# Two head groups' last query-weight rows in one block, no idle products between stages, and thirty small transfers in the queue

## The chip, the core and the metric

One core of a Trainium2 chip runs the whole kernel as one program. The metric is the device time of one execution in microseconds (us), the median of several runs; lower is better. The core has five engines that matter here: PE (TensorE, matrix products; PEld is its weight load), DVE (VectorE), ACT (ScalarE), POOL (GpSimd) and SP (SyncE), which in this kernel does nothing but issue transfers. The transfers themselves run on the core's 16 DMA engines.

## The reference

A decoder step of four tokens (B = 4) of width D = 448: pre-normalised attention against a cache, then a pre-normalised MLP.

```python
x = A_x                                             # (4, 1, 448)
h = x + attention(layernorm(x), k_cache, v_cache, wq, wo)
h2 = h + mlp(layernorm(h), w1, b1, w2, b2)          # returned

# attention: 16 query heads, 8 key/value heads, head size 256,
# only the last W = 1024 of 4096 cache positions are read
q = (x @ wq).reshape(4, 1, 16, 256)                 # wq is (448, 4096)
p = softmax(q . k / 16); o = p . v
return o.reshape(4, 1, 4096) @ wo                   # wo is (4096, 448)

# mlp: layernorm once more, gelu(y @ w1 + b1) @ w2 + b2, with 1792 hidden units
```

With four tokens there is little arithmetic. What is large is the data: every byte of the read cache positions and of the weights (all in float32) is used once, 88.23 MB read by the profile's count.

## The kernel before

The work is cut by the 8 key/value heads, called groups here. Each group needs its keys, its values, 512 columns of `wq` and 512 rows of `wo`. The host packs them into arrays, all but one with 128 rows (one for each partition of the on-chip memory), so that one transfer brings a block of long rows. There are three slots of on-chip memory (`ring`, line 213), used in turn: `t0`, `l1`, `l2`, `l3` and so on. Groups are treated in pairs ("stages" n = 0 to 3): `both_queries` projects the queries of both groups of a pair into one accumulator, `scores` multiplies them with the keys, `softmax` follows on DVE and ACT, `transpose_p` turns the probabilities, `values` multiplies them with the values, and `outputs` adds the product with `wo` to `acc`. Stage boundaries follow the transfers: after each load `l1` to `l8` the program computes what that load made possible. The last pair and the MLP (arrays `k7`, `vo`, `v7`, `wo`, `w1`, `w2`) form a tail with finer transfers: `w1` in two pieces, `w2` in four pieces of falling size.

Order and waits. The kernel is recorded by a small layer (`Machine`, line 78): each engine gets its instructions in the order in which the code is written, and each instruction waits for the semaphores of those it depends on. All transfers are issued by SP, in the order of the code, into one hardware queue. A transfer into a slot first waits until PE has read the slot's old contents. In the profile nearly every instruction has line 74, the layer's recording line, so one goes by names: `slot<-l` is a load of `l1` to `l8`; `b_s` are the scores, `b_o` the values' products (late in the program also the fill and the last products), `b_m` projections and transposes, `b_acc` the output products, `b_t` transposed probabilities and idle products.

The last 64 rows of `wq`. 448 is 3 times 128 plus 64. For one group, `packed` (line 740) puts the first 384 rows into three blocks of 512 columns, and the last 64 rows into a fourth block of 256 columns, its left half on partitions 0 to 63 and its right half on 64 to 127. So `wq_parts` (line 239) makes five products for a group: three of 512 columns, and two of 256 columns, for which the normalised input `yT` has an extra fifth chunk. Group 1 is different: its three full blocks come with `k0`, and its last 64 rows come by two transfers of their own, `wq1` into `wq1_last` (lines 457 to 460), 64 KB each, read from a source with 8 rows of 4 times 512 numbers each.

Idle products. `keep_warm_between` (line 444) runs six products of a zeroed bfloat16 tile into an unused accumulator. It stands behind seven of the stages (after `l1` to `l7`). Other idle and fill products (`keep_warm`, `fill`) stand in the tail.

Of the kernel before, what the change touches and what calls it, by code (L numbers as in the profile page):

```python
# [5 lines left out]
F32 = mybir.dt.float32  # L6
# [5 lines left out]
B, D = 4, 448  # L12
HQ, HKV, SK, DH = 16, 8, 4096, 256
# [3 lines left out]
P = 128  # L17
H = P // 2
ND = 4
# [3 lines left out]
Q = 32  # L23
CACHE = NKC * B * DH
HALF = CACHE // 2
WEIGHTS = 4 * D
SLOT = CACHE + 2 * WEIGHTS + HALF
COLUMNS = ND * B + 4 + 4 * 4
# [3 lines left out]
GRANULE = 4  # L32


class Memory:
# [9 lines left out]
    def part(self, ap):  # L45
        if self.psum:
            return slice(0, 1), np.zeros(1, int)
        pairs = list(ap.ap)
        first, at = divmod(ap.offset, self.row)
        rows = slice(first // GRANULE, -(-(first + pairs[0][1]) // GRANULE))  # L50
# [148 lines left out]

def block_kernel(nc, wq0, k0, wq1, l1, l2, l3, l4, l5, l6, l7, l8, k7, vo, v7, wo, w1, w2, out):  # L200
    real, nc = nc, Machine(nc)
# [53 lines left out]
    def output_weights(t):  # L255
# [6 lines left out]
        out=ident, in_=ident, compare_op=ALU.not_equal, fill=1.0, base=0, pattern=[[-1, P]], channel_multiplier=1  # L262
# [11 lines left out]

    yz = const.tile([P, ND + 1, B + Q], F32, name="yT")
    nc.vector.memset(yz, 0.0)
    yT = [yz[:, :, B:], yz[:, :, :Q]]
    wq1_last = const.tile([H, 512], F32, name="wq1_last")
    zT = const.tile([P, ND, Q], F32, name="zT")
# [42 lines left out]

    def project(pq, parts, start):
        for j, y, cols, w in parts:
            nc.tensor.matmul(
                pq[j * Q : (j + 1) * Q, cols], y, w,
                start=start and cols.start == 0, stop=not start and cols.stop == 512,
            )

# [123 lines left out]
    wqt, xT, b2T, b1T = cut(load(t, 0, wq0), (WEIGHTS, ND * B, 4, 4 * 4))  # L453
    wqt = wq_parts(yT[0], wqt)
    xT = xT.rearrange("p (a b) -> p a b", a=ND)
    ka, kb, wqt1 = cut(load(t, WEIGHTS + COLUMNS, k0), (HALF, HALF, 3 * 512))
    for i in range(2):
        nc.sync.dma_start(
            wq1_last[i * Q : (i + 1) * Q, :], wq1[i].rearrange("e (p c) -> e p c", c=512)[:, :4, :]
        )  # L460
    d = work.tile([P, ND, B], F32, tag="d", name="d_x")
# [7 lines left out]
    nc.vector.tensor_mul(yT[0][H:, 4, :B], d[H:, 3, :], rx[H:, :])  # L469
    pq = pq_tile(0)  # L470
    project(pq, wqt, True)

# [13 lines left out]

    project(pq, wq_parts(yT[1], wqt1, wq1_last), False)
    queries(0, pq)
# [22 lines left out]
    keep_warm_between()  # L511

# [3 lines left out]
    outputs(0, po, rec, (wo_a, wo_b))  # L516
    keep_warm_between()

    wq_a, wq_b, ka, kb, k2 = cut(load(slot("l3"), 0, l3), (WEIGHTS, WEIGHTS, HALF, HALF, HALF))
    both_queries(1, (wq_a, wq_b))  # L520
# [4 lines left out]
    keep_warm_between()  # L525

    k2, v, wq_a, wq_b = cut(load(slot("l4"), 0, l4), (HALF, CACHE, WEIGHTS, WEIGHTS))
    scores(s, 1, 1, keys(k2))
    p, sums = softmax(1, s)
    both_queries(2, (wq_a, wq_b))  # L530
    rec = transpose_p(1, p, sums)
    po = po_tile(1)
    values(0, chunks(v), po)
    keep_warm_between()

# [4 lines left out]
    outputs(1, po, rec, (wo_a, wo_b))  # L540
    keep_warm_between()

# [5 lines left out]
    rec = transpose_p(2, p, sums)  # L548
    keep_warm_between()

    v, va, wq_a, wq_b = cut(load(slot("l7"), 0, l7), (CACHE, HALF, WEIGHTS, WEIGHTS))
    po = po_tile(2)
    values(0, chunks(v), po)
    values(1, chunks(va), po, range(0, 2))
    both_queries(3, (wq_a, wq_b))
    keep_warm_between()

# [238 lines left out]
```

## Time and profile before

| what | value |
|---|---|
| time before, median of 3 runs | 211.98 us (211.97 to 212.29) |
| the profiled execution's own time | 212.03 us |
| its span, first to last instruction | 210.7 us |
| PE busy | 138.5 us (66%) |
| DVE busy, ACT busy | 28.8 us, 14.4 us |
| share of the time of 16 DMA engines taken by the main queue | 97.5% |
| bytes moved, mean rate over the span | 88.42 MB, 420 GB/s |
| mean granted TensorE clock | 0.862 |

The page lists, for each engine, how long it was busy, and for the DMA queue how long its packets took as a share of what 16 engines could have spent. The chain of waits goes back from the last instruction: at each step to what released it. A view by stretches of time ("windows") gives the same busy times and the DMA share for any part of the span. Issue rows (SPq) give when SP issued a transfer, and how long the issue took; landing times run from the issue to the last part on chip.

### The profile page before, as it was taken

Reading aid. Unit: us, or ns where it says so; the run is one execution under the profiler, and the core shown is the slowest. Engines: PE = TensorE matmul, PEld = TensorE weight load, DVE = VectorE, ACT = ScalarE, POOL = GpSimd, SP = SyncE. Lnnn points to the kernel's source line nnn. Section 1 sums busy time; section 2 is a strip of 40 time slices with the busy share of each in tenths; the row PEclk is TensorE's granted clock in tenths of the full one; section 3 lists DMA queues with packets and bytes.
Section 4 is the critical chain, followed back from the end, with each engine's and each line's share of the span. In section 5 each row is a group of like instructions: output and inputs, shape, how many; then the busy total and the mean of one; then the engine's idle time right before and its main releaser. Section 6 shows DMA issues by size and latency. Waiting matters only on the chain.

```text
span 210.7 us, 2189 instructions
## 1 busy us (share of the span) xinstructions
PE 138.5 (66%) x976; PEld 47.2 (22%) x976; DVE 28.8 (14%) x135; ACT 14.4 (7%) x34; POOL 5.0 (2%) x17
## 2 busy tenths in 40 slices
PE   0557869621971676098459577619806999888996
PEld 0420212200220221023112111202301223224332
DVE  7210101300020011013002003200100213012320
ACT  2010000200000010011000000200100002010311
POOL 5100000000000000000000000000000000000100
PEclk9999996985697599769969958757975899999999
DMA  7999999899999999999999999999999999999993
GB/s 296 428 399 473 448 491 389 386 411 530 398 398 410 530 389 410 410 518 398 413 411 448 481 398 437 398 494 398 446 392 448 416 428 429 437 398 452 412 410 131
DMA packets 3256, 88.42 MB, mean 420 GB/s; under 512 B 368, under 2 KB 624, under 8 KB 1200
## 3 DMA queue, kind: packets, MB, share of 16 engines
q1 hardware_dynamic: 3248, 88.30, 97.5%
q8 instruction: 7, 0.11, 0.2%
q14 instruction: 1, 0.01, 0.0%
HBM read 88.23 MB, written 0.07 MB: 419 GB/s over the span
## 4 chain that ended last, share of the span: by engine, by line
DMA 78%; PE 17%; SPq 2%; DVE 1%; issue 1%; ACT 0%
DMA slot<-l 64%; DMA slot<-w 14%; PE b_o L74 9%; PE b_s L74 4%; PE b_acc L74 3%; SPq L74 2%; PE b_m L74 1%; DVE oT L74 1%; DVE w_o L74 0%; PE b_t L74 0%; DVE o_u L74 0%; ACT o_u L74 0%; DVE o_res L74 0%
## 5 line engine op out<-in xcount | busy, mean ns | idle before, releaser
L74 PE MATMUL b_o<-slot,pT 128*32 128x512 f32 x224 | 32.3, 729 | 26.3 <-DMA slot<-l 25.6
L74 PE MATMUL b_s<-slot,qT 128*32 128x512 f32 x256 | 38.7, 760 | 14.3 <-DMA slot<-l 12.9
L74 PE MATMUL b_m<-slot,yT 128*32 128x512 f32 (+1 forms) x76 | 11.4, 705 | 11.4 <-DMA slot<-l 6.2
L74 PEld LDWEIGHTS b_s<-slot,qT 128*32 128x32 f32 x256 | 9.4, 136 | 40.8 <-issue 23.9
L74 PEld LDWEIGHTS b_o<-slot,pT 128*32 128x32 f32 x224 | 7.7, 130 | 47.5 <-DMA slot<-l 28.0
L74 PE MATMUL b_t<-idle 128*32 128x512 bf16 x64 | 17.7, 397 | 0.5 <-DVE pT L74 0.5
L74 DVE TENSOR_REDUCE w_mx<-b_s 128x1 f32<-128x512 f32 x8 | 5.5, 691 | 49.5 <-PE b_s L74 49.5
L74 ACT ACTIVATE o_p<-b_s,w_nm 128x512 f32<-128x512 f32 x8 | 5.4, 682 | 96.4 <-DVE w_nm L74 96.4
L74 DVE TENSOR_SCALAR w_o<-b_o,w_rec 128x512 f32<-128x512 f32 x4 | 3.0, 751 | 50.2 <-PE b_o L74 50.2
L74 PEld LDWEIGHTS b_m<-slot,yT 128*32 128x32 f32 x76 | 4.2, 140 | 17.8 <-DMA slot<-l 6.7
L74 PEld LDWEIGHTS b_t<-idle 128*32 128x32 bf16 x64 | 5.9, 99 | 9.9 <-issue 5.2
L74 PE MATMUL b_t<-ident,o_p 128*128 128x128 f32 x32 | 5.0, 283 | 4.0 <-ACT o_p L74 3.9
L74 PE MATMUL b_acc<-slot,oT 128*32 128x448 f32 x52 | 6.1, 546 | 1.9 <-DVE oT L74 1.9
L74 DVE TENSOR_REDUCE w_sm<-b_m 128x32 f32<-128x128 f32 x4 | 1.2, 291 | 44.8 <-PE b_m L74 44.8
L74 ACT COPY w_qs<-b_m 128x512 f32<-128x512 f32 x4 | 2.3, 584 | 58.0 <-PE b_m L74 58.0
L74 POOL TENSOR_TENSOR o_r<-w_ve,mhalf 128x1 f32<-128x1 f32 x2 | 1.1, 542 | 189.3 <-DVE w_ve L74 189.3
L74 PEld LDWEIGHTS b_t<-ident,o_p 128*128 128x128 f32 x32 | 3.4, 141 | 7.4 <-ACT o_p L74 7.4
L74 PE MATMUL b_m<-ident,w_qs 128*128 128x128 f32 x16 | 3.1, 324 | 3.0 <-ACT w_qs L74 3.0
L74 PE MATMUL b_m<-slot,mean 128*128 128x12 f32 (+1 forms) x4 | 1.1, 371 | 5.4 <-DMA slot<-wq 5.4
L74 PE MATMUL b_o<-slot,yT 128*32 128x512 f32 x10 | 4.6, 595 | 0.0
L74 PE MATMUL b_m<-ident,w_o 128*128 128x128 f32 x20 | 3.3, 287 | 1.8 <-DVE w_o L74 1.8
L74 DVE COPY pT<-b_t 128x16 f32<-128x16 f32 x32 | 3.3, 167 | 5.9 <-PE b_t L74 5.9
(94 smaller groups left out, 66.3 us busy)
## 6 DMA issues: line engine op xcount, KB each, us to landing
slot<-l SPq DMA_DIRECT2D x6, 7936.0 KB, 43.7
slot<-l SPq DMA_DIRECT2D x2, 6144.0 KB, 35.3
slot<-k SPq DMA_DIRECT2D x1, 4864.0 KB, 15.7
slot<-vo SPq DMA_DIRECT2D x1, 4544.0 KB, 32.9
slot<-k SPq DMA_DIRECT2D x1, 4096.0 KB, 40.9
slot<-v SPq DMA_DIRECT2D x1, 3072.0 KB, 18.8
slot<-w SPq DMA_DIRECT2D x1, 2240.0 KB, 28.4
slot<-w SPq DMA_DIRECT2D x1, 1792.0 KB, 33.8
```

The source lines that it names most:

```text
L74: self.machine.add(Op(self.name, lambda: getattr(issuer, what)(*args, **kwargs), outs, ins, what))
```

## The change

Three things are changed.

- **Query weights.** The last 64 rows of both groups of a pair are now stacked into one block of 128 rows and 512 columns (`last`). `yT` loses its fifth chunk; its fourth chunk now holds the last 64 inputs on partitions 0 to 63 in the columns of the first group and on partitions 64 to 127 in those of the second, so one product (`wq_last`) serves both groups. A pair takes 7 products instead of 10. For pair 0 the block comes with `wq0`, which grows from 1828 to 2084 columns. `wq1`, `wq1_last` and their two transfers are gone. The number of bytes of the weights is the same.
- **Idle products.** `keep_warm_between` and its seven calls are gone, 42 products.
- **Small transfers.** `spread` issues 15 transfers: of 15 rows with 19 numbers, 14 rows with 18, and so on to 1 row with 5, from `l1` into an otherwise unused tile `aside`. It is called after the load of `k0`, and again after the two pieces of `w1` and before those of `w2`. POOL clears `aside` near the end, which makes it wait for the second fifteen; what POOL had to do before that is done by then in program order, and no other instruction waits for this clearing.

A fourth edit makes the recording layer's bookkeeping of partitions use the step of an access as well as its count.

```diff
-    def wq_parts(y, t, last=None):
-        parts = [(a, y[:, a, :], slice(0, 512), t[:, a * 512 : (a + 1) * 512]) for a in range(3)]
-        if last is not None:
-            return parts + [(3, y[:H, 3, :], slice(0, 512), last)]
-        for i in range(2):
-            parts.append((3, y[:, 3 + i, :], slice(i * 2 * P, (i + 1) * 2 * P), t[:, 3 * 512 :]))
-        return parts
+    def wq_parts(y, t):
+        return [(a, y[:, a, :], t[:, a * 512 : (a + 1) * 512]) for a in range(3)]
+
+    def wq_last(t):
+        return [(3, yT[0][:, 3, :], t)]
...
-    def keep_warm_between():
-        warm = ps_t.tile([P, 512], F32, tag="t", name="between")
-        keep_warm(6, warm)
...
+    aside = const.tile([16, 180], F32, name="aside")
+
+    def spread():
+        at = 0
+        for n in range(15, 0, -1):
+            nc.sync.dma_start(aside[:n, at : at + 4 + n], l1[:n, : 4 + n])
+            at += 4 + n
...
-    ka, kb, wqt1 = cut(load(t, WEIGHTS + COLUMNS, k0), (HALF, HALF, 3 * 512))
-    for i in range(2):
-        nc.sync.dma_start(
-            wq1_last[i * Q : (i + 1) * Q, :], wq1[i].rearrange("e (p c) -> e p c", c=512)[:, :4, :]
-        )
+    ka, kb, wqt1 = cut(load(t, QUERY + 512 + COLUMNS, k0), (HALF, HALF, QUERY))
+    spread()
...
         for g in range(2):
-            project(pq, wq_parts(yT[g], wqs[g]), g == 0)
+            project(pq, wq_parts(yT[g], wqs[g]), g == 0, g == 1)
+        project(pq, wq_last(wqs[2]), True, True)
         queries(n, pq)
...
     w1t = cut(load(e[0], CACHE, w1, (2 * F + F // 2, F)), (F, F, F // 2, F))
+    spread()
     w2t = cut(load(e[2], CACHE, w2, (8 * D, 3 * D, 2 * D, D)), NFC * (D,))
...
+    nc.gpsimd.memset(aside, 0.0)
```

On SP at the start of the program, where `wq`, `k` and `l` are the loads of `wq0`, `k0` and of `l1`, `l2`, there stood before:

```order
L74 DMA slot<-wq 128x1828 [waits barrier_Pool_Activation_PE_DVE_SP_release]
L74 DMA slot<-k 128x9728
L74 DMA wq_last<-wq 32x1x512 x2
L74 DMA slot<-l 128x12288
L74 DMA slot<-l 128x15872
```

With the change the start of SP's order is:

```order
L76 DMA slot<-wq 128x2084 [waits barrier_Pool_Activation_PE_DVE_SP_release]
L76 DMA slot<-k 128x9728
L76 DMA aside<-l 15x19
L76 DMA aside<-l 14x18
L76 DMA aside<-l 13x17
...
L76 DMA aside<-l 2x6
L76 DMA aside<-l 1x5
L76 DMA slot<-l 128x12288
L76 DMA slot<-l 128x15872
```

Fifteen issues, none of which waits, stand ahead of `l1` where two stood before.

On SP in the tail, where the two pieces of `w1` are followed by the first of `w2` (3584 columns), stands with the change:

```order
L76 DMA slot<-w 128x1792
L76 DMA aside<-l 15x19 [waits landed_28]
L76 DMA aside<-l 14x18 [waits landed_29]
...
L76 DMA aside<-l 2x6 [waits landed_41]
L76 DMA aside<-l 1x5 [waits landed_42]
L76 DMA slot<-w 128x3584
L76 DMA slot<-w 128x1344 [waits done_PE]
```

Each of the fifteen waits for its namesake of the first call, since it writes the same place; before, the row of 3584 columns followed the one of 1792 directly.

On PE after the outputs of pair 0 (`b_acc`), where the load of `l3` is waited for, there stood before:

```order
L74 MATMUL b_acc<-slot,oT 32x448 x3
L74 MATMUL b_t<-idle 32x512 x6
L74 MATMUL b_m<-slot,yT 32x512 [waits landed_191]
L74 MATMUL b_m<-slot,yT 32x512 x2
L74 MATMUL b_m<-slot,yT 32x256 x2
L74 MATMUL b_m<-slot,yT 32x512 x3
L74 MATMUL b_m<-slot,yT 32x256 x2
```

and with the change:

```order
L76 MATMUL b_acc<-slot,oT 32x448 x3
L76 MATMUL b_m<-slot,yT 32x512 [waits landed_190]
L76 MATMUL b_m<-slot,yT 32x512 x6
L76 MATMUL b_m<-ident,w_qs 128x128 [waits done_ACT]
```

The six idle products ahead of the wait are gone, and the ten projections behind it are seven.

More of the change, by code (lines that the diff above doesn't have):

```diff
@@ L26 @@
 WEIGHTS = 4 * D
+QUERY = 3 * 512
 SLOT = CACHE + 2 * WEIGHTS + HALF
@@ L49, in part @@
         first, at = divmod(ap.offset, self.row)
-        rows = slice(first // GRANULE, -(-(first + pairs[0][1]) // GRANULE))
+        end = first + pairs[0][0] // self.row * (pairs[0][1] - 1) + 1
+        rows = slice(first // GRANULE, -(-end // GRANULE))
         cols = np.zeros(1, int)
@@ L197, in tile, with block_kernel @@
         return flat.rearrange(f"p ({names}) -> p {names}", **{f"a{i}": n for i, n in enumerate(shape[1:])})
-def block_kernel(nc, wq0, k0, wq1, l1, l2, l3, l4, l5, l6, l7, l8, k7, vo, v7, wo, w1, w2, out):
+def block_kernel(nc, wq0, k0, l1, l2, l3, l4, l5, l6, l7, l8, k7, vo, v7, wo, w1, w2, out):
     real, nc = nc, Machine(nc)
@@ L320, in rsqrt, with project @@
         nc.gpsimd.tensor_tensor(dst, ve, mhalf[: dst.shape[0], : dst.shape[1]], op=ALU.pow)
[L323 to L327, printed above, removed]
-            )
+    def project(pq, parts, start, stop):
+        for j, y, w in parts:
+            nc.tensor.matmul(pq[j * Q : (j + 1) * Q], y, w, start=start, stop=stop)
     def pq_tile(n):
@@ L442, in keep_warm @@
             nc.tensor.matmul(warm[:Q], idle[:, :Q], idle, start=True, stop=True)
[L444 to L446 removed]
     def po_tile(g, pool=ps_o, tag="o"):
         return pool.tile([P, 2, DH], F32, tag=tag, name=f"po{g}")
+    aside = const.tile([16, 180], F32, name="aside")
[4 more added lines that the diff above has]
+            at += 4 + n
     t = slot("t0")
[L453 to L454 removed]
+    wqt, wq_both, xT, b2T, b1T = cut(load(t, 0, wq0), (QUERY, 512, ND * B, 4, 4 * 4))
     xT = xT.rearrange("p (a b) -> p a b", a=ND)
[L456 to L460 removed]
+    ka, kb, wqt1 = cut(load(t, QUERY + 512 + COLUMNS, k0), (HALF, HALF, QUERY))
+    spread()
     d = work.tile([P, ND, B], F32, tag="d", name="d_x")
@@ L468, in block_kernel @@
     nc.vector.tensor_mul(yT[0][:H, 3, :B], d[:H, 3, :], rx[:H, :])
-    nc.vector.tensor_mul(yT[0][H:, 4, :B], d[H:, 3, :], rx[H:, :])
+    nc.vector.tensor_mul(yT[0][H:, 3, B : 2 * B], d[H:, 3, :], rx[H:, :])
     pq = pq_tile(0)
-    project(pq, wqt, True)
+    project(pq, wq_parts(yT[0], wqt), True, False)
+    project(pq, wq_last(wq_both), True, True)
     wide = t[:, SLOT - 6 * P :].rearrange("p (n j q) -> p n j q", n=6, j=4)
@@ L516, in block_kernel @@
     outputs(0, po, rec, (wo_a, wo_b))
-    keep_warm_between()
-    wq_a, wq_b, ka, kb, k2 = cut(load(slot("l3"), 0, l3), (WEIGHTS, WEIGHTS, HALF, HALF, HALF))
-    both_queries(1, (wq_a, wq_b))
+    wq_a, wq_b, wq_c, ka, kb, k2 = cut(load(slot("l3"), 0, l3), (QUERY, QUERY, 512, HALF, HALF, HALF))
+    both_queries(1, (wq_a, wq_b, wq_c))
     s = score_tiles(1)
@@ L524, in block_kernel @@
     scores(s, 1, 0, keys(k2))
-    keep_warm_between()
-    k2, v, wq_a, wq_b = cut(load(slot("l4"), 0, l4), (HALF, CACHE, WEIGHTS, WEIGHTS))
+    k2, v, wq_a, wq_b, wq_c = cut(load(slot("l4"), 0, l4), (HALF, CACHE, QUERY, QUERY, 512))
     scores(s, 1, 1, keys(k2))
     p, sums = softmax(1, s)
-    both_queries(2, (wq_a, wq_b))
+    both_queries(2, (wq_a, wq_b, wq_c))
     rec = transpose_p(1, p, sums)
@@ L540, in block_kernel @@
     outputs(1, po, rec, (wo_a, wo_b))
-    keep_warm_between()
     kb, ka, k2 = cut(load(slot("l6"), 0, l6), (HALF, HALF, HALF))
@@ L548, in block_kernel @@
     rec = transpose_p(2, p, sums)
-    keep_warm_between()
-    v, va, wq_a, wq_b = cut(load(slot("l7"), 0, l7), (CACHE, HALF, WEIGHTS, WEIGHTS))
+    v, va, wq_a, wq_b, wq_c = cut(load(slot("l7"), 0, l7), (CACHE, HALF, QUERY, QUERY, 512))
     po = po_tile(2)
@@ L745, in packed @@
         return np.concatenate([full, last], axis=-1)
-    wq = packed(np.asarray(A_wq).reshape(D, HKV, 512).transpose(1, 0, 2))
+    wq = np.asarray(A_wq).reshape(D, HKV // 2, 2, 512)
+    whole = wq[: 3 * P].reshape(3, P, HKV // 2, 2, 512).transpose(2, 3, 1, 0, 4).reshape(HKV, P, QUERY)
+    last = wq[3 * P :].transpose(1, 2, 0, 3).reshape(HKV // 2, P, 512)
+    wq = [np.concatenate([whole[2 * n], whole[2 * n + 1], last[n]], axis=1) for n in range(HKV // 2)]
     wo = np.asarray(A_wo).reshape(HKV, 4, P, D).transpose(0, 2, 1, 3).reshape(HKV, P, 4 * D)
@@ L761 @@
     loads = {f"l{i + 1}": np.concatenate(parts, axis=1) for i, parts in enumerate(loads)}
-    k0 = np.concatenate([k[0], wq[1][:, : 3 * 512]], axis=1)
-    wq1 = np.asarray(A_wq).reshape(D, HKV, 512)[3 * P :, 1].reshape(2, 8, 4 * 512)
-    wq1 = np.concatenate([wq1, np.zeros((2, 8, 512), np.float32)], axis=2)
+    k0 = np.concatenate([k[0], whole[1]], axis=1)
     vo = np.concatenate([v[6], wo[6, :, : 2 * D]], axis=1)
@@ L782 @@
     arrays = {
-        "wq0": np.concatenate([wq[0], xT, b2, b1], axis=1), "k0": k0, "wq1": wq1, **loads, "k7": k[7], "vo": vo, "v7": v[7], "wo": wo_end, "w1": w1, "w2": w2,
+        "wq0": np.concatenate([whole[0], last[0], xT, b2, b1], axis=1), "k0": k0, **loads, "k7": k[7], "vo": vo, "v7": v[7], "wo": wo_end, "w1": w1, "w2": w2,
     }
```

16 lines of the change are left out of this document (6 added, 10 removed).

## The prediction

> **What bounds the kernel now.** First the page, for which resource is full.
>
> ```profile
> span 210.7 us, 2189 instructions
> PE 138.5 (66%) x976; PEld 47.2 (22%) x976; DVE 28.8 (14%) x135; ACT 14.4 (7%) x34; POOL 5.0 (2%) x17
> q1 hardware_dynamic: 3248, 88.30, 97.5%
> q8 instruction: 7, 0.11, 0.2%
> DMA 78%; PE 17%; SPq 2%; DVE 1%; issue 1%; ACT 0%
> ```
>
> The main queue takes 97.5% of what 16 DMA engines have, 205.4 us of 210.7; no compute engine comes near. So I read the DMA share by stretches of time (columns: stretch, length, PE, PEld, DVE, ACT and POOL busy, TensorE clock, DMA share, GB/s).
>
> ```profile
> 0.00:1.70 1.70, 0.00 (x0) 0.00 (x0) 0.55 (x4) 0.97 (x1) 1.10 (x8) 1.00 0.00 0
> 17.00:100.00 83.00, 52.35 (x330) 16.34 (x334) 8.66 (x46) 4.54 (x11) 0.00 (x0) 0.84 1.00 432
> 100.00:200.00 100.00, 71.99 (x520) 23.68 (x513) 12.83 (x57) 6.09 (x15) 0.83 (x2) 0.85 0.99 428
> 206.00:206.50 0.50, 0.50 (x12) 0.10 (x4) 0.00 (x0) 0.00 (x0) 0.00 (x0) 1.00 0.89 351
> 206.50:207.00 0.50, 0.50 (x20) 0.27 (x16) 0.00 (x0) 0.02 (x1) 0.00 (x0) 1.00 0.49 197
> 207.00:207.50 0.50, 0.50 (x24) 0.29 (x12) 0.00 (x0) 0.50 (x1) 0.00 (x0) 1.00 0.47 183
> 207.50:208.00 0.50, 0.50 (x21) 0.36 (x21) 0.00 (x0) 0.01 (x1) 0.00 (x0) 1.00 0.26 97
> 208.00:209.00 1.00, 0.73 (x24) 0.24 (x15) 0.19 (x1) 0.00 (x0) 0.00 (x0) 1.00 0.00 0
> ```
>
> Nothing moves for the first 1.7 us; then the engines run without a gap at 432 GB/s, 27.0 GB/s each. At the end the share falls in two steps: half of the engines stop near 206.5, the other half go on until about 207.9. The late half sets the end, since a transfer has landed when its last engine is done:
>
> ```profile
> 207.94 0.79 PE L74 MATMUL b_o<-slot,gT_last 128*4 128x64 f32 x16
> 208.34 0.11 PEld L74 LDWEIGHTS b_o<-slot,gT_last 128*4 128x4 f32 x8 [0.21 <-DMA slot<-w]
> 208.81 0.29 DVE L74 TENSOR_TENSOR o_res<-b_o,o_hb 128x128 f32<-128x128 f32 x1 [4.40 <-PE b_o L74]
> 209.13 0.35 SPq L74 DMA_DIRECT2D out<-o_res  x1
> ```
>
> The last products wait for the last piece of `w2`; half a microsecond later the sum and the output transfer follow. So the time is the finish of the latest engine plus a tail of about 2.8 us. Anything else counts only if it leaves the queue empty.
>
> **The change, part by part.**
>
> *Idle products and fewer projections.* The queue runs far ahead of PE. From the chain of waits (start, us, what), and two issue rows:
>
> ```profile
> 62.94 44.94 DMA slot<-l
> 117.41 42.44 DMA slot<-l
> 168.93 0.80 SPq L74 DMA_DIRECT2D slot<-v  x2
> slot<-v SPq DMA_DIRECT2D x1, 3072.0 KB, 18.8
> ```
>
> A load issued at 62.94 lands 44.9 us later, but its 7,936 KB (8.13 MB) need only 18.8 us at 432 GB/s; so it stood 26 us in the queue, and PE may free a slot that much later. At 117.41 it is 23.6 us. The tightest is `v7`: 18.8 us for 3.15 MB that need 7.3, so 11.5 us. Against that:
>
> ```profile
> 151.32 1.47 PE L74 MATMUL b_t<-idle 128*32 128x512 bf16 x6
> 159.89 3.64 PE L74 MATMUL b_o<-slot,pT 128*32 128x512 f32 x16 [7.10 <-DMA slot<-l]
> 180.50 3.64 PE L74 MATMUL b_o<-slot,pT 128*32 128x512 f32 x32 [0.54 <-DMA slot<-vo]
> ```
>
> After six idle products PE waits 7.10 us, and its next 16 products take 228 ns each where, after a wait of 0.54 us, 32 take 114 ns each. The clock is lost in the wait with the idle products as it will be without them. If one more stage went cold, 16 products would cost 1.8 us, inside 11.5. I cost both edits at 0; the cover is that slack.
>
> The Trainium skill's "TensorE: Matmul & The Clock Gate", Part 1, says that the clock halves after an idle window of about 3.4 us, which speaks against taking idle products out; the trace agrees on the halving, 228 against 114 ns, and by the rule the 7.10 us wait is cold either way.
>
> *Query weights on the engines.* The two removed transfers are 64 KB each, 131 KB together; the bytes now ride with `wq0`, which has 128 rows. At 27.0 GB/s that is 0.30 us on each of 16 engines. Read from 8 source rows, they lay either on 8 engines, 0.61 us on each of those, or on 16. So a late engine gets +0.30 (it had none), -0.30 (it had them), or 0. Which engines are late is the question. One cause is seen around 36 us:
>
> ```profile
> q8 instruction: 1, 0.02, 4.2%
> ```
>
> In the 1.4 us from 35.5 to 36.9 one instruction fetch takes 4.2% of 16 engines' time: 0.94 us of one engine. There are seven of these and one more on another queue, about as many as there are late engines. No row says which engines fetch. With fetches on engines that also carried the small parts I would expect a third step of 0.61 us in the fall of the share; I see two. So I take the side of the cost, at half its size: +0.15.
>
> The skill's "DMA: Bandwidth & Descriptors", section on why a DMA increments its semaphore by 16, says that a transfer runs on the largest number up to 16 that divides both sides' outer sizes, on the lowest-numbered engines: 8 for the removed pair, n for a small transfer of n rows. No row here shows the numbers of engines.
>
> *Small transfers on the engines.* The nearest row is the output, 128 packets of 512 B and 16 semaphore writes in 0.5 us:
>
> ```profile
> DMA packets 144, 0.07 MB, mean 131 GB/s; under 512 B 16, under 2 KB 144, under 8 KB 144
> q1 hardware_dynamic: 144, 0.07, 46.8%
> ```
>
> 46.8% of 16 times 0.5 us is 3.74 us, 26 ns a packet; 19 of them are 512 B at 27.0 GB/s, 7 ns are fixed. A row of 20 to 76 B is then 10 ns, with its semaphore write 17. An engine that has a row of all thirty gets 0.51 us, one with none 0; if each packet cost the full 26 ns, 1.56. On average an engine has 240 / 16 = 15 rows, 0.26 us. I take 0.20 for the late ones.
>
> *SP's time.* Issues (start, us they took), their durations (min/median/max ns), and landings after the issue:
>
> ```profile
> 0.74 0.39 SPq L74 DMA_DIRECT2D slot<-wq  x1
> 1.18 0.41 SPq L74 DMA_DIRECT2D slot<-k  x1
> 1.64 1.55 SPq L74 DMA_DIRECT2D wq_last<-wq  x2
> 170.25 0.96 SPq L74 DMA_DIRECT2D slot<-w  x2
> L74 SPq DMA_DIRECT2D wq_last<-wq x2: 682/750/819, 1.6 to 2.5; - x2
> L74 SPq DMA_DIRECT2D slot<-l x8: 327/328/499, 3.2 to 117.4; - x8
> slot<-k SPq DMA_DIRECT2D x1, 4864.0 KB, 15.7
> slot<-w SPq DMA_DIRECT2D x1, 896.0 KB, 30.1
> ```
>
> Fifteen issues at 0.33 to 0.82 us are 4.9 to 12.3 us, so `l1` is issued between 6.5 and 13.9 instead of 1.64 + 1.55 = 3.2. `k0` occupies the queue until 1.2 + 15.7 = 16.9, and first bytes came 1.0 us after the first issue (0.74 to 1.7): hidden by at least 2 us. In the tail, where the two pieces of `w1` are issued from 170.25 to 171.2, the fifteen end by 171.2 + 12.3 = 183.5 while the second piece lands at about 170.7 + 30.1 = 200.8: hidden. Both at 0.
>
> *Fewer instructions.* 42 idle products and 22 others of PE go, each with a weight load: 128 of 1952 instructions. Seven fetches for 1952 make one per 260 to 280, so at most one fetch fewer; the end is set by the latest of eight engines, and seven remain. 0, at best -0.94.
>
> **The sum**, against the profiled execution: 212.03 + 0.15 + 0.20 = 212.4. The median lies 0.05 under the profiled time, so **212.3 us**. This case alone spans 211.7 (-0.30, no cost of small rows) to 213.2.
>
> **Rivals.**
>
> *A. The queue takes a limited number of transfers (slower).* The last piece of `w2` took 7.34 us to issue:
>
> ```profile
> 172.73 7.34 SPq L74 DMA_DIRECT2D slot<-w  x1
> slot<-k SPq DMA_DIRECT2D x1, 4096.0 KB, 40.9
> slot<-vo SPq DMA_DIRECT2D x1, 4544.0 KB, 32.9
> ```
>
> `k7`, issued at 128.7, had landed by then (169.6). Nine others were outstanding (`vo`, two of `v7`, `wo`, two of `w1`, three of `w2`), and it was let in at 180.07, when `vo`, issued at 147.50, was ending. If nine is the limit whatever their size, the fifteen fill the queue behind `k0`: when it ends the last six and `l1` are still to be issued, 7 times 0.4 to 0.75 us plus 1.0 for first bytes, 3.8 to 6.3 us of empty engines, and the same again before `w2`. That is +7.6 to +12.6, about 221 us. Against it: `vo` landed at 147.50 + 32.9 = 180.4, after the issue had ended, so the limit is not on transfers that have not landed; a limit on queued rows fits too (eight whole transfers of 8 rows per engine, 64), and 30 small rows beside two or six large transfers pass it without a gap. It decides if fewer than 16 transfers may wait behind `k0`.
>
> *B. The issue is dearer than any row shows (slower).* From 1.64 to 16.2 there are 14.6 us for fifteen: it decides from 0.97 us each. At 1.2, `l1`'s first bytes come at 20.6 instead of 17.2: +3.4, 215.4. The dearest row is 0.82.
>
> *C. The late half moves up (faster).* If the late engines are those that carried the small parts (-0.30), the last fetch falls behind the last load, and small rows lie on the engines that have time, the second step shrinks from 1.4 us towards the mean, 0.7: 211.3. For it: the share shows that half the engines idle 1.4 us at the end. Against it: no part of the change takes a fetch off a late engine before the last.
>
> *D. The clock counts after all.* If `l8`'s stage went so cold that `v7` came 11.5 us later, +1.8 for the next cold 16 products: 214. Only the 7.10 us wait speaks on it, and against it.
>
> **How the numbers follow.** A measurement here tells 0.2%, 0.42 us, from no change. The forecast's case has 0.60: of it 0.40 within 0.42 us, 0.18 slower, 0.02 faster. C has 0.22, 0.19 of it faster. A 0.10, B 0.06 and D 0.02 are slower. Together: faster 0.21, same 0.43, slower 0.36. The range 211.2 to 213.8 leaves out A, nearly all of B, and the far end of C, 0.18.
>
> **What would show it.** Right: the DMA share stays 1.00 from 5 to 200 us; `l1` is issued before 14 us; the share still falls in two steps, ending near 208.3; PE's waits before loads grow by about 1.5 us and nothing else moves. Wrong: a share under 0.9 around 17 us or 200 us (A or B, told apart by whether the small issues take long from the first or only from the eighth); a single step at the end (C); a `v7` issued after 180 us (D).

## The result, and the profile after

The changed kernel takes 215.82 us (median of 4 runs, 215.18 to 216.56) against 212.09 us before (211.97 to 212.29). The ratio is 1.0178, 95% interval 1.016 to 1.0197: slower by 3.7 us, and outside the predicted range of 211.2 to 213.8. The profiled execution is the fastest of the four, 215.18 us, with a span of 213.9 us.

The page after (engines, queues, and the chain by engine):

```profile
span 213.9 us, 2100 instructions
PE 130.2 (61%) x912; PEld 41.8 (20%) x912; DVE 28.8 (13%) x135; ACT 14.4 (7%) x34; POOL 5.2 (2%) x18
q1 hardware_dynamic: 3648, 88.31, 97.0%
q8 instruction: 7, 0.11, 0.2%
DMA 73%; PE 15%; SPq 9%; issue 1%; DVE 1%
```

PE has 8.3 us less to do and the bytes are the same, yet the span is 3.2 us longer. The DMA engines are still the bound. The end of the kernel after, first by stretches (columns as in the prediction, DMA share and GB/s last), then its last waits and products:

```profile
208.00:208.50 0.50, 0.21 (x4) 0.19 (x8) 0.00 (x0) 0.00 (x0) 0.00 (x0) 1.00 0.88 348
208.50:209.00 0.50, 0.50 (x8) 0.13 (x4) 0.00 (x0) 0.00 (x0) 0.00 (x0) 1.00 0.51 204
209.50:210.00 0.50, 0.50 (x16) 0.17 (x12) 0.00 (x0) 0.00 (x0) 0.00 (x0) 1.00 0.28 111
210.00:210.50 0.50, 0.50 (x24) 0.40 (x16) 0.00 (x0) 0.45 (x1) 0.00 (x0) 1.00 0.18 68
210.50:211.00 0.50, 0.50 (x18) 0.20 (x16) 0.00 (x0) 0.09 (x1) 0.00 (x0) 1.00 0.09 32
211.00:211.50 0.50, 0.50 (x21) 0.29 (x19) 0.00 (x0) 0.00 (x0) 0.00 (x0) 1.00 0.00 0
```

```profile
208.29 1.71 PE L76 MATMUL b_acc<-slot,gT 128*32 128x448 f32 x16 [1.96 <-DMA slot<-w]
211.09 0.80 PE L76 MATMUL b_o<-slot,gT_last 128*4 128x64 f32 x16
212.28 0.35 SPq L76 DMA_DIRECT2D out<-o_res  x1
```

Before, the share fell in two steps and was gone by 208.0. After, half of the engines stop at about 208.5, and from there it runs down a staircase: 0.51, 0.28, 0.18, 0.09. That is eight late engines, then about four, three, one or two. The last of them finishes near 211. PE waits 1.96 us for the first piece of `w2`, a wait that was too short to be listed before. The last products start at 211.09 instead of 207.94, 3.15 us later, and the tail behind them is 2.8 us as it was. So the loss lies in when the data arrive.

Where did it arise? The share of busy time doesn't tell, but the bytes do. Two stretches that hold the two sets of small transfers, before and then after:

```profile
15.00:22.00 7.00, 4.36 (x11) 0.97 (x12) 0.00 (x0) 0.58 (x1) 0.00 (x0) 1.00 1.00 431
198.00:206.00 8.00, 7.52 (x63) 2.89 (x65) 1.76 (x7) 1.75 (x5) 1.08 (x2) 1.00 1.00 421
```

```profile
15.00:22.00 7.00, 3.24 (x14) 1.10 (x18) 0.70 (x5) 0.59 (x1) 0.00 (x0) 1.00 1.06 407
198.00:206.00 8.00, 7.54 (x58) 3.01 (x56) 2.21 (x10) 2.69 (x7) 1.33 (x3) 1.00 1.00 373
```

All four have a share of 1.00 or above. But the second stretch moved 373 GB/s instead of 421: 48 times 8 us is 0.38 MB less, 0.9 us of all engines at 432 GB/s. So the time that was lost counts as busy. (The view puts a packet with all its bytes and all its time where the packet starts, and a packet of a large load takes up to 2.3 us, so such a stretch can be some per cent off and a share can pass 1.00. Where it matters below, a figure from the trace's packet records is given, in which each packet is spread over its own duration.)

What SP did in the kernel after (issue rows: start, us; then durations of the thirty, min/median/max ns; then KB and us from issue to landing), and PE's waits for loads:

```profile
1.62 5.60 SPq L76 DMA_DIRECT2D aside<-l  x15
7.26 0.83 SPq L76 DMA_DIRECT2D slot<-l  x2
172.05 11.60 SPq L76 DMA_DIRECT2D aside<-l  x15
183.70 9.75 SPq L76 DMA_DIRECT2D slot<-w  x4
L76 SPq DMA_DIRECT2D aside<-l x30: 253/341/2688, 1.6 to 182.8; - x30
slot<-l SPq DMA_DIRECT2D x1, 6144.0 KB, 26.4
slot<-w SPq DMA_DIRECT2D x1, 1792.0 KB, 24.5
161.08 3.64 PE L76 MATMUL b_o<-slot,pT 128*32 128x512 f32 x16 [8.89 <-DMA slot<-l]
```

`l1` is issued at 7.26 and lands at 7.26 + 26.4 = 33.7; before it was 3.23 + 28.5 = 31.7. So it comes 1.9 us later though it was issued long before its turn. `l8` ended PE's wait at 161.08 instead of 159.89, 1.2 us later: of the first delay 0.7 us is made up again on the way. The first piece of `w2` lands at 183.70 + 24.5 = 208.2.

### The profile page after: what moved, and what is told of

Its sections match the earlier page's. It is cut to its first block, busy times and chain, and to the rows that moved or that the text cites. A ratio compares the mean times of both kernels' runs of the same rounds, so it can differ in the third digit from the quotient of the medians.

```text
span 213.9 us, 2100 instructions
## 1 busy us (share of the span) xinstructions
PE 130.2 (61%) x912; PEld 41.8 (20%) x912; DVE 28.8 (13%) x135; ACT 14.4 (7%) x34; POOL 5.2 (2%) x18
## 4 chain that ended last, share of the span: by engine, by line
DMA 73%; PE 15%; SPq 9%; issue 1%; DVE 1%
DMA slot<-l 61%; DMA slot<-w 11%; SPq L76 9%; PE b_o L76 9%; PE b_acc L76 3%; PE b_s L76 2%; PE b_m L76 1%; DVE oT L76 1%; DVE w_o L76 0%; DVE o_res L76 0%
## 5 line engine op out<-in xcount | busy, mean ns | idle before, releaser
L76 PE MATMUL b_o<-slot,pT 128*32 128x512 f32 x224 | 34.3, 768 | 31.1 <-DMA slot<-l 30.2
L76 PE MATMUL b_s<-slot,qT 128*32 128x512 f32 x256 | 39.1, 766 | 17.4 <-DMA slot<-l 16.0
L76 PE MATMUL b_m<-slot,yT 128*32 128x512 f32 x56 | 11.7, 839 | 12.8 <-DMA slot<-l 7.8
L76 PE MATMUL b_t<-idle 128*32 128x512 bf16 x22 | 6.6, 382 | 0.0
L76 PEld LDWEIGHTS b_m<-slot,yT 128*32 128x32 f32 x56 | 2.3, 137 | 18.7 <-DMA slot<-l 8.6
L76 PEld LDWEIGHTS b_m<-ident,w_qs 128*128 128x128 f32 x16 | 2.3, 179 | 8.6 <-ACT w_qs L76 8.6
## 6 DMA issues: line engine op xcount, KB each, us to landing
slot<-w SPq DMA_DIRECT2D x1, 1792.0 KB, 24.5
```

The source lines that it names most:

```text
L76: self.machine.add(Op(self.name, lambda: getattr(issuer, what)(*args, **kwargs), outs, ins, what))
```

## The experiments

The theory formed on the trace of after: each small transfer holds every engine that it uses for a fixed time of about 0.2 us, whatever its rows (their landings step by about that much). What was still to be told apart was which part of the change costs what, whether it goes by transfers, by rows or by the length of a row, and what the query block and the idle products do by themselves. Each time stands beside runs of the kernel before on the same chip (212.00 to 212.12).

### Without the small transfers, and with one set of them

The changed kernel without both calls:

```diff
-    spread()
...
-    spread()
...
-    nc.gpsimd.memset(aside, 0.0)
```

> The changed kernel without its thirty small transfers: the query block and the missing idle products alone. Theory S (the small transfers are the whole loss, each holding an engine for about 0.19 us, as their landings 17.41, 17.59, 17.79 ... 19.98 us step): 211.7 to 212.4 us, like before. Rival Q (the bytes moved to all engines and the colder PE are part of the loss, the 1.15 us by which every load between l2 and w1 lands later): 213.1 to 213.6 us.

Measured: 212.71 us (7 runs), ratio 1.0029 [1.0017, 1.004]. The small transfers cost 215.82 - 212.71 = 3.1 us of the 3.7; the rest of the change costs 0.6, more than was expected. The wait for the first piece of `w2` is nearly gone:

```profile
206.36 1.71 PE L76 MATMUL b_acc<-slot,gT 128*32 128x448 f32 x16 [0.19 <-DMA slot<-w]
```

With the second call alone:

```diff
     ka, kb, wqt1 = cut(load(t, QUERY + 512 + COLUMNS, k0), (HALF, HALF, QUERY))
-    spread()
```

> The changed kernel with the fifteen small transfers before w2 alone. Theory S: the loads up to w1 land as before, the four pieces of w2 2 us later: 213.9 to 214.4 us. Rival Q: loads up to w1 already 1.15 us late, 215.0 to 215.6 us.

With the first call alone:

```diff
     w1t = cut(load(e[0], CACHE, w1, (2 * F + F // 2, F)), (F, F, F // 2, F))
-    spread()
...
-    nc.gpsimd.memset(aside, 0.0)
```

> The changed kernel with the fifteen small transfers behind k0 alone. Theory S: l1 lands 2 us late, l2 and all later loads 1.1 to 1.2 us late, because some of the instruction fetches then fall on engines that are ahead: 213.0 to 213.5 us. Rival Q: the same time, but for another reason, which the run without any small transfers tells apart. Rival D (delays add in full, nothing is absorbed): 214.0 to 215.0 us.

Measured: 213.8 us (ratio 1.0089 [1.0056, 1.0122]) and 213.71 us (1.0074 [1.0059, 1.0089]). Each call alone costs 1.0 to 1.1 us, both together 3.1; both times lie just outside what theory S had said (213.9 to 214.4 and 213.0 to 213.5). The five runs of the second call alone spread from 213.21 to 215.35, so its price is known to about half a microsecond at best. The stretches show the same loss of bytes, and it stands where the call is. Without small transfers, with the first call alone (15 to 22), with the second alone (198 to 206):

```profile
15.00:22.00 7.00, 2.91 (x10) 0.87 (x10) 0.55 (x5) 0.71 (x2) 0.00 (x0) 0.71 1.05 456
198.00:206.00 8.00, 7.54 (x57) 3.00 (x56) 2.14 (x9) 2.69 (x7) 1.09 (x2) 1.00 0.99 412
```

```profile
15.00:22.00 7.00, 3.04 (x10) 0.91 (x10) 0.56 (x5) 0.59 (x1) 0.00 (x0) 0.65 1.02 399
```

```profile
198.00:206.00 8.00, 7.07 (x54) 2.60 (x52) 1.98 (x9) 2.08 (x5) 1.33 (x3) 1.00 0.99 368
```

456 - 399 over 7 us is 0.40 MB, 0.92 us of all engines; 412 - 368 over 8 us is 0.35 MB, 0.81 us. With the packets spread over their durations it is 434 against 382 and 421 against 380 GB/s, 0.84 and 0.76 us. A set of fifteen takes that much on the average engine.

The small transfers put into the kernel before, with nothing else of the change but the bookkeeping line. The first call stands behind the two transfers of `wq1`, the second between `w1` and `w2`:

```diff
...
+    spread()
...
+    spread()
...
+    nc.gpsimd.memset(aside, 0.0)
```

> The kernel before with the thirty small transfers added at the same two places, nothing else changed. Theory S: 214.8 to 216.2 us, about as slow as the changed kernel. Rival Q: 213.5 to 214.3 us, less than the changed kernel, since query block and idle products are as before.

Measured: 215.96 us, ratio 1.0196 [1.0142, 1.0251]. The small transfers alone bring a loss as large as that of the whole change. The four runs lie between 215.22 and 217.88, so whether the block's 0.6 us comes on top cannot be seen here. PE's wait for `w2` is there too:

```profile
208.32 1.71 PE L75 MATMUL b_acc<-slot,gT 128*32 128x448 f32 x16 [1.53 <-DMA slot<-w]
```

### By the row, by its length, or by the transfer?

The first set alone, with rows of 512 B instead of 20 to 76 B, into a free stretch of the slot `t0`:

```diff
...
-        at = 0
-        for n in range(15, 0, -1):
-            nc.sync.dma_start(aside[:n, at : at + 4 + n], l1[:n, : 4 + n])
-            at += 4 + n
+        for i in range(15):
+            n = 15 - i
+            at = 11840 + i * 128
+            nc.sync.dma_start(t[:n, at : at + 128], l1[:n, i * 128 : (i + 1) * 128])
...
```

> The fifteen small transfers behind k0 alone (none before w2), of 15 to 1 rows again, but each row 512 bytes long instead of 76 to 20, into a free stretch of slot t0. Theory S (a fixed time for each transfer on an engine, whatever its rows): they land about 0.2 us apart as the short ones did, l1 at 33.0 to 33.9 us, 213.3 to 213.9 us. Rival P (rows under 512 bytes are what is dear): they land 0.03 to 0.08 us apart, and the time is that without small transfers, 212.5 to 212.9 us.

Measured: 213.81 us, ratio 1.0084 [1.0071, 1.0097], beside 213.71 and 1.0074 [1.0059, 1.0089] with the short rows. The length of a row makes no difference that can be told; short rows are not the cause.

The first set as one transfer of 128 rows:

```diff
...
-        at = 0
-        for n in range(15, 0, -1):
-            nc.sync.dma_start(aside[:n, at : at + 4 + n], l1[:n, : 4 + n])
-            at += 4 + n
+        nc.sync.dma_start(aside, l1[:, :20])
...
```

> In place of the fifteen small transfers behind k0 one transfer of 128 rows of 80 bytes, 8 rows for each of 16 engines; none before w2. Theory S: one fixed time of 0.2 us, 212.6 to 213.0 us, l1 at 32.2 to 32.6. Rival R (each small row costs the 0.19 us, not each transfer): 8 times 0.19, l1 at 33.5 to 34 us, 214.0 to 214.5 us.

Measured: 212.86 us, ratio 1.0041 [1.0028, 1.0054], beside 212.71 and 1.0029 [1.0017, 1.004] with none: at most 0.3 us more, and not to be told from nothing. Yet it has more rows than the fifteen together (128 against 120). Its issue, its landing and `l1`'s:

```profile
1.63 0.42 SPq L76 DMA_DIRECT2D aside<-l  x1
2.09 1.13 SPq L76 DMA_DIRECT2D slot<-l  x2
aside<-l SPq DMA_DIRECT2D x1, 10.0 KB, 15.7
slot<-l SPq DMA_DIRECT2D x1, 6144.0 KB, 29.6
15.00:22.00 7.00, 3.47 (x14) 1.11 (x18) 0.70 (x5) 0.58 (x1) 0.00 (x0) 0.63 1.07 457
```

It lands at 1.63 + 15.7 = 17.3, with 8 rows an engine as early as the first of the fifteen in the next run with one (17.4). The stretch moves 457 GB/s as without it, and `l1` lands at 2.09 + 29.6 = 31.7. So the cost goes by transfers, not by rows. The Trainium skill advises the same: the section "Rules for kernel authors" of "DMA: Bandwidth & Descriptors" says to join many small transfers into a large one, because under 64 KB one pays mostly overhead.

The first set with 16 rows in each of the fifteen, so that every engine can get one row of every transfer:

```diff
-            nc.sync.dma_start(aside[:n, at : at + 4 + n], l1[:n, : 4 + n])
+            nc.sync.dma_start(aside[:, at : at + 4 + n], l1[:16, : 4 + n])
...
```

> Fifteen small transfers behind k0, none before w2, but each of 16 rows, so that every engine has a row of all fifteen and no engine is ahead of another. Theory S (a fixed time of each transfer on each engine it uses, and the lag of uneven rows partly absorbed by engines that are ahead): 15 times 0.19 us on every engine, 2.8 us over the kernel without small transfers, 215.2 to 215.9 us. Rival M (what costs is the slowest engine alone, which has 15 rows here and there): 213.5 to 214.0 us, as with 15 to 1 rows.

Measured: 214.69 us, ratio 1.0125 [1.0111, 1.0139]: 2.0 us over the kernel without small transfers and 1.0 us over the set with 15 to 1 rows. The direction is as expected, the size smaller. The stretch, the issues, and the landings of the first and the last of the fifteen:

```profile
15.00:22.00 7.00, 3.34 (x14) 1.11 (x18) 0.70 (x5) 0.58 (x1) 0.00 (x0) 1.00 1.02 324
1.61 7.02 SPq L76 DMA_DIRECT2D aside<-l  x15
7.75 0.88 SPq L76 DMA_DIRECT2D aside<-l  x2
aside<-l SPq DMA_DIRECT2D x1, 1.2 KB, 15.8
aside<-l SPq DMA_DIRECT2D x1, 0.3 KB, 12.0
```

The first lands at 1.61 + 15.8 = 17.4. The last, issued at about 8.2, lands at about 20.2: fourteen steps of 0.20 us. The bytes give less. With the packets spread over their durations the stretch moved 312 GB/s against 434 without small transfers: 0.85 MB, 2.0 us of all engines, 0.13 us for each transfer on each engine. The time, 2.0 us over fifteen, agrees with that.

The packets show where this time stands. The main queue while the small transfers pass, first a stretch with small packets alone, then one with all of them and the first row of `l1` on each of the 16 engines; last the same first rows behind the one transfer of 128 rows (16.3 to 17.5):

```profile
q1 hardware_dynamic: 147, 0.00, 46.5%
q1 hardware_dynamic: 512, 0.80, 311.3%
q1 hardware_dynamic: 176, 0.80, 160.8%
```

46.5% of 16 times 0.2 us (16.4 to 16.6) is 1.49 us for 147 small packets, 10 ns each. The two others differ by 150.5% of 16 times 1.2 us (16.4 to 17.6 with the fifteen), 28.9 us, or 1.8 us an engine, and the small packets make little of that. What is longer is the packet behind them: the first row of `l1` takes 2.7 to 4.0 us on each engine, where it takes 1.8 behind the one transfer. So by either count a small transfer costs an engine 0.12 to 0.13 us here, its rows pass in 10 ns each, and its price is paid by the load packet that follows. Whether it is the semaphore write that ends a transfer or something else in it, no run separates. Nor was it tried whether it matters that the small rows of each set all go to the same 15 or 16 partitions, while the one transfer goes to 128.

Nor is the price the same for each transfer. The fifteen rows of a set differ in length, and an engine's small packets follow one another at 12 to 14 ns, so the packet records tell how many rows of a set each engine had. Behind the second set of the changed kernel a row of `w2` takes 0.54 to 0.55 us on the engines with up to seven small rows, and 0.70, 0.87, 1.05, 1.20, 1.36, 1.54, 1.80 and 1.94 us on those with eight to fifteen. The run with the second set alone gives the same within 0.05 us. There about seven transfers are hidden behind the next row, and each further one costs 0.14 to 0.26 us.

### The idle products and the query block

The kernel before without the seven calls of idle products, of which the diff shows one:

```diff
-    keep_warm_between()
```

> The kernel before without its 42 idle products between stages, query weights and transfers as before. It looks for the 0.6 us that the changed kernel keeps without its small transfers. Theory W (the weights' 131 KB now also lie on the engines that end last, +0.30 to +0.6): no difference here, 211.9 to 212.3 us. Rival I (colder products, or instruction fetches that fall elsewhere because PE has fewer instructions): 212.5 to 212.9 us.

Measured: 212.05 us (11 runs), ratio 1.0004 [0.9995, 1.0012]. Nothing.

The changed kernel without small transfers, with the idle products back (`keep_warm_between` and its calls as in the kernel before), so that only the query block is left:

```diff
-    spread()
...
+    keep_warm_between()
```

> The query block alone: the changed kernel without small transfers and with the 42 idle products back. Theory W: 212.4 to 212.9 us, as without the idle products. Rival I: 211.9 to 212.3 us.

Measured: 212.88 us, ratio 1.0045 [1.0031, 1.0058]. The block by itself costs 0.6 to 0.9 us. Four runs asked why, since moving 131 KB from eight engines to sixteen is 0.30 us by the bytes. First, the kernel before with the two transfers of `wq1` read from 16 rows instead of 8:

```diff
-            wq1_last[i * Q : (i + 1) * Q, :], wq1[i].rearrange("e (p c) -> e p c", c=512)[:, :4, :]
+            wq1_last[i * Q : (i + 1) * Q, :], wq1[i].rearrange("e (p c) -> e p c", c=512)[:, :2, :]
...
-    wq1 = np.asarray(A_wq).reshape(D, HKV, 512)[3 * P :, 1].reshape(2, 8, 4 * 512)
-    wq1 = np.concatenate([wq1, np.zeros((2, 8, 512), np.float32)], axis=2)
+    wq1 = np.asarray(A_wq).reshape(D, HKV, 512)[3 * P :, 1].reshape(2, 16, 2 * 512)
+    wq1 = np.concatenate([wq1, np.zeros((2, 16, 512), np.float32)], axis=2)
```

> The kernel before, with one thing changed: the two transfers of 64 KB with group 1's last query rows read from a source of 16 rows instead of 8, so that they can lie on 16 engines, as the bytes do in the changed kernel; their number, their place and their bytes stay. Theory W (the query block costs because 131 KB move from half of the engines to all of them): the engines that are late at the end get 0.30 us more, as much as the changed block gives them, so the time rises by most of what the block alone cost (212.88 us with the idle products): 212.4 to 212.9 us, and k0 lands within 0.5 us of 16.93. Rival P (the cost comes from something else in the block: the wider first transfer, its place ahead of k0): no change, 211.9 to 212.2 us.

Measured: 212.99 us, ratio 1.0038 [1.0024, 1.0051]. The page counts 3264 packets in the main queue instead of 3248. Rows and bytes are the same, so these are eight more semaphore writes for each of the two transfers, which lie on 16 engines now and lay on 8 before. The time is just above what theory W expected, and `k0` is not where it should be: it lands at 1.18 + 16.8 = 18.0, 1.1 us late (row below). In this kernel, and with the block, the arrays behind can also lie elsewhere in the chip's memory. Three runs separate that: the kernel before with a longer padding of `wq1` alone; the block alone with a padding of `k0`; the 16 rows with a shorter padding.

```diff
-    wq1 = np.concatenate([wq1, np.zeros((2, 8, 512), np.float32)], axis=2)
+    wq1 = np.concatenate([wq1, np.zeros((2, 8, 1024), np.float32)], axis=2)
```

> The kernel before, with only the padding of the two query transfers' source changed, from 512 to 1024 unused numbers a row: no transfer, instruction or size differs, but every array behind it can lie 32 KB further on in the chip's memory, as in the run in which the source had 16 rows. Theory P (part of what the query block costs comes from where the arrays lie, not from the engines): the time moves away from 212.05, to 212.3 to 213.0 us, and the engines that are done early at the end are late too. Theory W (it is the engines' bytes alone): no change, 211.9 to 212.2 us.

```diff
...
-    k0 = np.concatenate([k[0], whole[1]], axis=1)
+    k0 = np.concatenate([k[0], whole[1], np.zeros((P, 64), np.float32)], axis=1)
```

> The query block alone, with the idle products (212.88 us), and 64 unused numbers added to each row of k0's source that are not loaded, so that the sum of the arrays ahead of l1 is what it was in the kernel before. Theory P: the arrays from l1 on lie where they lay, and the time falls to 212.0 to 212.5 us. Theory W: unchanged, 212.6 to 213.1 us.

```diff
...
-    wq1 = np.concatenate([wq1, np.zeros((2, 16, 512), np.float32)], axis=2)
+    wq1 = np.concatenate([wq1, np.zeros((2, 16, 256), np.float32)], axis=2)
```

> The kernel before with the two query transfers read from 16 rows (212.99 us), but with a padding that keeps the source at its size in the kernel before. Theory P: the loss of 0.9 us shrinks to what the bytes alone give, 0.3 us: 212.2 to 212.5 us. Theory W: unchanged, 212.8 to 213.1 us.

Measured: 212.06 us (ratio 0.9998 [0.999, 1.0007]), 212.78 (1.0031 [1.0019, 1.0044]) and 212.85 (1.0034 [1.0022, 1.0047]). All three are as theory W had said: the place in memory is not the cause, and bytes that move from half of the engines to all are enough for a loss of this size. But the two kernels lose it at different places. The first stretches of the kernel before (with the landing of `wq0`), of the block alone, and of the 16 rows:

```profile
1.00:5.00 4.00, 0.00 (x0) 0.00 (x0) 3.43 (x15) 1.01 (x1) 2.48 (x9) 1.00 0.98 370
slot<-wq SPq DMA_DIRECT2D x1, 914.0 KB, 4.6
```

```profile
1.00:5.00 4.00, 0.00 (x0) 0.00 (x0) 3.43 (x15) 1.01 (x1) 2.48 (x9) 1.00 0.80 280
15.00:22.00 7.00, 3.04 (x10) 0.91 (x10) 0.51 (x4) 0.58 (x1) 0.00 (x0) 1.00 1.05 454
slot<-wq SPq DMA_DIRECT2D x1, 1042.0 KB, 5.2
slot<-l SPq DMA_DIRECT2D x1, 6144.0 KB, 30.5
```

```profile
1.00:5.00 4.00, 0.00 (x0) 0.00 (x0) 3.25 (x15) 1.01 (x1) 2.58 (x9) 1.00 0.98 368
15.00:22.00 7.00, 3.77 (x8) 0.38 (x8) 0.00 (x0) 0.16 (x1) 0.00 (x0) 1.00 1.01 384
slot<-k SPq DMA_DIRECT2D x1, 4864.0 KB, 16.8
```

With the block the view gives the first four microseconds 280 GB/s instead of 370, but most of that is where it puts the packets. Spread over their durations it is 250 against 267 GB/s: 0.07 MB, 0.16 us of all engines. `wq0` comes 0.6 us later and `l1` 0.4: 1.64 + 30.5 = 32.1, against 31.7. The bytes alone are 0.30 us on an engine that had none of them; with the 0.16 they make 0.46, about what `l1` is late. A further 0.3 us comes late in the run: from 100 to 206 us the load packets are longer by that much on the average engine than in the kernel before (0.54 us over their shortest times, against 0.22). Together this is about 0.8, an estimate that fits the 0.6 to 0.9 measured. With the 16 rows the start is as before, and the loss is behind `k0`: 47 GB/s less over 7 us, 0.76 us. There the first row of `l1` takes 2.0 to 2.8 us on every engine instead of 1.8, so here two transfers are enough to make the packet behind them longer; read from 8 rows, on 8 engines, they were not (1.8 us behind them). Why that is so, and why the load packets are longer late in the run with the block, stays open.

### Can the early half take the end?

Half of the engines are done 1.4 us early in the kernel before. If they were the eight lowest-numbered, a last piece of `w2` on these alone would end sooner. The last 448 columns by four transfers of 32 rows, each from a source with 8 rows, and the control with the same four from 32 rows (shown as it differs from the first):

```diff
...
-    w2t = cut(load(e[2], CACHE, w2, (8 * D, 3 * D, 2 * D, D)), NFC * (D,))
+    w2t = cut(load(e[2], CACHE, w2, (8 * D, 3 * D, 2 * D)), 13 * (D,))
+    w2t.append(e[2][:, CACHE + 13 * D : CACHE + 14 * D])
+    for i in range(4):
+        nc.sync.dma_start(
+            w2t[13][i * Q : (i + 1) * Q, :], w2d[i].rearrange("e (p c) -> e p c", c=D)[:, :4, :]
+        )
...
```

> The kernel before, with the last piece of w2 (448 columns, 229 KB) brought by four transfers of 32 rows from a source with 8 outer rows, as the two small parts of the query weights are, so that 8 engines should carry all of it: 0.53 us more on them, 0.53 less on the others. Theory H (the engines that end last are mostly those that did not carry the query parts): the last piece lands 0.3 to 0.5 us earlier, 211.4 to 211.8 us. Rival L (the late engines are mixed): the late ones among the eight end 0.5 us later, 212.3 to 212.7 us.

```diff
...
-            w2t[13][i * Q : (i + 1) * Q, :], w2d[i].rearrange("e (p c) -> e p c", c=D)[:, :4, :]
+            w2t[13][i * Q : (i + 1) * Q, :], w2d[i].rearrange("e (p c) -> (e p) c", c=D)
...
```

> The same four transfers of 32 rows with a source of 32 outer rows, so that 16 engines carry each: the control for cutting one transfer into four. Both theories: 2 rows of 1792 bytes are 0.14 us an engine, under the fixed 0.19 us of a transfer, so 4 times 0.19 instead of 0.57: 212.1 to 212.5 us.

Measured: 212.81 us (1.0031 [1.0018, 1.0043]) and 212.9 us (1.0036 [1.0023, 1.0049]). Both lose 0.7 to 0.8 us to the kernel before, more than either theory had said, and the eight engines gain nothing over sixteen. The share at the end of the first of them:

```profile
207.50:208.00 0.50, 0.50 (x22) 0.20 (x11) 0.00 (x0) 0.27 (x1) 0.00 (x0) 1.00 0.18 68
208.50:209.00 0.50, 0.27 (x11) 0.00 (x0) 0.00 (x0) 0.00 (x0) 0.00 (x0) 1.00 0.05 18
```

A staircase again: about three engines are busy at 207.7 and one at 208.7, where only the four last transfers are left. So late engines are among those eight, in this kernel early and late ones are mixed, and three more transfers at the end cost more than was there to gain.

None of these kernels is faster than the one before; the one without idle products equals it (212.05).

## Why the prediction was wrong

**The step that failed is "small transfers on the engines".** It priced them by the row: 10 ns for a row and 7 ns for its semaphore write, from the output's 26 ns a packet, 0.20 us in all and 1.56 at most. The 10 ns were right for the rows themselves (10 ns a small packet). What it had no term for is a price by the transfer, paid by the packet behind: 0.13 us on each engine it uses (fifteen with 16 rows: 2.0 us of all engines), the same for rows of 20 to 76 B and of 512 B, and next to nothing for one transfer of 128 rows. Thirty came to 3.1 us. The nearest row was a poor one: the output is a single transfer with nothing behind it, and from it a cost that falls once per transfer, on what follows, cannot be read.

The upper bound fell with it. It took each packet at the dearest price seen, but left out that a transfer may cost time beside its own packets. The output's rows gave no reason against that.

**Why both sets cost more than twice one.** The share before showed half of the engines done 1.4 us early. An engine among these gives nothing to the end until its slack is used up. With the second set alone, the packet records show the engines that have seven to fifteen rows of it arriving there at 198.7 to 199.8 us, and those with up to six at 200.7 to 201.0. The loaded ones are about 1.7 us ahead, and fifteen transfers cost at most 1.6. With both sets, the engines with eight to fifteen rows arrive 1.4 to 2.2 us later, at 200.2 to 201.6, and those with up to six as before. So the same engines lose twice, the first set uses up the slack, and the second falls on the end. In the profiled executions one set costs 0.3 us or less (213.24 us without, 213.49 with the first, 213.21 with the second) and both 1.9 (215.18); the medians, 1.0 to 1.1 and 3.1, have the same shape. Fifteen on all engines find no slack and give their 2.0 in full. The Trainium skill's "DMA: Bandwidth & Descriptors", section on why a DMA increments its semaphore by 16, says that a transfer takes the largest number of engines up to 16 that divides both sides' outer sizes, the lowest-numbered ones, by which n rows lie on the same n engines each time. The staircase at the end agrees, engine after engine with fewer transfers; no row shows the engines' numbers.

**"Query weights on the engines"** had the right sign and was mis-sized: +0.15 with ends at 0.30, measured 0.6 to 0.9. It counted the bytes on a late engine and nothing else; the runs show a further 0.16 us at the start and 0.3 in longer load packets. Nor do the engines run at 432 GB/s from the first byte on, as it says: from 1.7 to 5.0 us before, the packets spread over their durations give 1.07 MB, 324 GB/s.

**"Idle products and fewer projections", 0:** right, 1.0004 [0.9995, 1.0012]. PE's wait grew from 7.10 to 8.89 us, as was said, and the products behind it are as cold as before (3.64 us).

**"SP's time", 0:** right. The first set was issued in 5.60 us, `l1` at 7.26, inside the stated 6.5 to 13.9. Of the second set the first ten went as fast, and then SP was held (chain of the kernel after; start, us):

```profile
175.57 0.29 SPq L76
175.91 1.86 SPq L76
180.03 2.69 SPq L76
```

So there is a limit, but `w2` was still issued at 183.70, when `w1` was 18 us from landing.

**"Fewer instructions", 0:** right; still seven fetches.

**The rivals.** A (a limit of nine transfers) and B (issues of 0.97 us and more) fell: fifteen small ones went into the queue behind two large ones within 5.60 us. C (the late half moves up) and D (the clock) did not happen. The right answer, a price by the transfer on the engine, was not among the rivals; at 215.8 us it looked from outside like B.

**What would show it.** The DMA share stayed at 1.00, which the text had down as "right". That sign was blind: the longer packets count as busy. Of the signs it named, the fall in two steps ending near 208.3 failed, since it became a staircase to 211; the GB/s of the same stretches would have shown the loss, but were not named.

## What to carry to other kernels

Count transfers, not only bytes and rows: in a queue that is never empty small transfers took about 0.13 us each from every engine they lay on, and joining fifteen into one took the cost away. Where the DMA engines are the bound, read the GB/s beside the share, since the share counts an engine as busy while a packet is held up, and take stretches that are long against one packet. And look at how unevenly the engines end before pricing something by its average: what falls on engines with slack is cheap until the slack is gone, and then costs in full.

## What the hardware showed unexpectedly

- Fifteen transfers of at most 1.2 KB on all engines took 2.0 us of all 16 engines, with landings 0.20 us apart. Their packets of at most 76 B took 10 ns each; the time stood in the load packet behind them.
- On one engine about seven small transfers were hidden behind the next row of `w2`; each further one made that row 0.14 to 0.26 us longer.
- SP's queue had eighteen transfers outstanding by 8.1 us without holding SP (`k0`, fifteen small ones, `l1`, `l2`), yet in the tail held it for 1.86 us with sixteen outstanding (six loads and ten small ones). So its limit is not one on the number of transfers.
- In the first 3.3 us of traffic the engines moved 324 GB/s where they later moved 432.
- Spreading two 64 KB transfers over 16 engines instead of 8 made the kernel 0.7 to 0.9 us slower with the same bytes and the same number of transfers, in two runs.
